# First token group of an mLSTM and SwiGLU kernel: its own results in two halves of 64 tokens, and a new order ahead of the feed-forward part

## The chip, the cores and the metric

The kernel runs on one core of a Trainium2 chip. A core has five engines that run side by side, each with its own queue of instructions: TensorE (PE: matmuls and transposes, results into PSUM), VectorE (DVE), ScalarE (ACT), GpSimd (POOL) and SyncE (SP, which here only issues DMAs). They wait for one another by semaphores. The metric is the device time of one execution in microseconds (us); all times are in us where nothing else is said.

## What is computed

Two blocks in sequence, all in float32. The first is an mLSTM cell over 4 batches, 8 heads, 768 tokens and head dimension 40; the second is a SwiGLU feed-forward over the 3072 tokens with 320 features.

```python
for t in range(S):                                   # S = 768, for all batches and heads
    m_new = np.maximum(f_gate[:, :, t] + m, i_gate[:, :, t])
    f_stab = np.exp(f_gate[:, :, t] + m - m_new)
    i_stab = np.exp(i_gate[:, :, t] - m_new)
    m = m_new
    C = f_stab[..., None, None] * C + i_stab[..., None, None] * np.einsum('bhd,bhe->bhde', vt, kt)
    n = f_stab[..., None] * n + i_stab[..., None] * kt
    h_tilde = np.einsum('bhde,bhe->bhd', C, qt)
    denom = np.maximum(np.abs(np.einsum('bhd,bhd->bh', n, qt)[:, :, None]), 1.0)
    y[:, :, t] = sigmoid(o_gate[:, :, t]) * h_tilde / denom
x = y.transpose(0, 2, 1, 3).reshape(B * S, H * D)    # 3072 x 320
g = x @ w_gate                                       # 320 x 1536
out = (g * sigmoid(g) * (x @ w_val)) @ w_out         # 1536 x 320
```

The weights of the feed-forward arrive as 64-bit floats and are turned into 32-bit floats on the chip.

## The kernel before

**Groups and stages.** The 768 tokens are cut into 6 groups of 128 tokens, and the recurrence becomes matrix products: a group's result is the part that its own tokens give each other (a masked 128 x 128 matrix of weights for every batch and head) and a part from the state C that earlier groups left. Group 0 has no earlier state, so it needs its own part alone. A group's results, transposed (`xT`), feed `hidden` (L646), which makes twelve slices of 128 of the 1536 hidden features, and `project` or `project_all`, which multiply by w_out. From the first `hidden` on, TensorE works on the feed-forward of one group, and the cell of the next group is put between its slices. What lies ahead of the first `hidden` is the cell of group 0 and the conversion of the first pieces of the weights. The change is almost wholly there, in L567 to L614.

**Pairs.** The 32 combinations of batch and head (`BH`) are worked on in two halves P = 0 and 1, each of two batches u = 2P and 2P + 1 with 8 heads.

**Group 0, in the order of its functions:**
- `first_mask`, `first_inputs`, `first_maxima` (L478 to L490) sum the logarithms of the decay weights in eight PSUM banks; `first_exp` takes exp of them into `W0[s, t]` (128 source tokens s on the partitions, 128 result tokens t). For s > t the weight is 0. `W0` lies in the buffer `h_sb`, which the hidden features use later, and which takes weight pieces in between.
- `first_turn` (L504) transposes k or q of one half, 128 tokens at a time: eight transposes of 128 x 128 in two banks, and a copy from each bank to SBUF, on the engines given. `turn_one` (L291), which later groups use, does the same 64 tokens at a time, with 64-row transposes, and copies each half of the tokens.
- `first_values` (GpSimd) weights v by the last column of `W0` for the state that group 0 leaves. It must come ahead of `first_scores` of the same half.
- `first_scores` multiplies q and k in 64 matmul records over both halves, and VectorE multiplies them into `W0` (L523).
- `first_own(u)` multiplies `W0` by v for the 8 heads of a batch, over all 128 source tokens, into the bank `first_y` (L530). Column 41 of v is 1 and gives the denominator.
- `first_x(u)` on VectorE divides, `sig(P)` on ScalarE takes the sigmoid of the output gate, `first_gate(P)` multiplies by it and copies 64 columns behind the row.
- `first_seam(P)` transposes the two batches' results (five blocks each, three banks) and copies them into `xT(0)`.
- `first_state(P)` multiplies k and the weighted v (L552), and `first_kept` copies the product to the state buffer.

**Weights.** `piece_load(p)` issues the DMAs of piece p of the weights, the w_gate half on SP's queue and the w_val half on ScalarE's for the first five pieces. Pieces 0 and 1 go to buffers of their own; piece 2 goes to part of `h_sb` and so waits until `first_own(2)` has read `W0` there. `convert(j)` is `scale(j)` (two ops on ScalarE, the upper and the lower word), `join(j)` (two on VectorE) and `rounded(j)` (one, on VectorE or GpSimd).

**`late_sums`** (L273) sums the forget gates of the later groups (a scan on VectorE, and a memset and a subtraction on GpSimd); `late_maxima`, after the first slice of `hidden`, uses it. **`burn(n)`** issues n matmuls of constants, whose results nobody reads.

**What sets the order.** The order of the calls is the order in each engine's queue; nothing is rescheduled. PSUM has eight banks under two names, "cell" and "gen", four each, given out in turn: a new tile waits until the readers of the fourth last one of its name are done. `hidden` takes its banks from "gen".

## Time and profile before

| | us |
|---|---|
| median of 3 runs (552.24 to 552.7) | 552.34 |
| the profiled execution | 551.99 |
| its span, first to last instruction | 550.0 |
| first matmul of `hidden` starts | 32.04 |
| `first_own` of batch 0, 1, 2, 3 starts | 14.49, 18.63, 23.09, 25.23 |
| scores of the first and the second half start | 12.44, 20.44 |
| first and second seam start on TensorE | 26.93, 29.45 |
| o_gate issues of both halves (SP) | 14.44 to 19.38 |
| w_gate and w_val halves of piece 0 issued | 19.43, 18.40 |
| piece 2 issued, on both queues | 25.04 |

The page of a profile gives busy time by engine, then the span in 40 slices, the DMA queues, the chain of work that ended last, and groups of instructions (line, engine, operation, what it writes and reads, shape, count, busy time and mean duration, idle time before it and what ended it). "PEld" is the loading of weights into TensorE's array, which overlaps its matmuls. A matmul in float32 leaves two records, a transpose one. Matmuls are pipelined, so that the ends in the records are modelled: the starts say how fast they follow each other. The timeline merges consecutive records of one line; its columns are start, length, engine and line, operation and operands, shape and count.

Slices of the page's second part, the first tenth of the span in the first four digits:

```profile
PE   8999999999999999999999999999999999999997
PEld 4964556774555575545575545576455567444475
DVE  5778668961346232455421545531436621111100
ACT  4376755352110133011024101115110100111100
POOL 2304265673011060011133011124001100000000
```

## The change

- `first_own` makes each head's product in two parts: result tokens 64 to 127 from all 128 source tokens, and result tokens 0 to 63 from source tokens 0 to 63 (the rest of their weights is 0). There are 16 matmuls for a batch instead of 8.
- The second half's k and q are turned by `turn_one`, k into banks of the name "gen".
- `first_own(1)` stands between these two turns, `first_x(0)` behind both.
- `piece_load(1)` follows `piece_load(0)`, ahead of `sig(0)`.
- `first_state(0)` moves from behind the second seam to ahead of the first, into a "gen" bank.
- The first half's gate goes to GpSimd; `sig(1)` and the second half's gate stand behind the first bank of the first seam.
- `late_sums` moves behind `convert(1)`; `rounded(0)` moves ahead of the second seam; both state copies are on ScalarE.
- The burns are 3, 2, 2, 2 and 5 instead of 3, 2 and 1.
- `scale` is written as two functions that are called one after the other, as before.

```diff
-    def turn_one(P, src, dst, engs):
-        tp = [bank("tp_kq").rearrange("p (a t) -> p a t", t=SUB) for _ in range(2)]
+    def turn_one(P, src, dst, engs, tag="cell"):
+        tp = [bank("tp_kq", tag).rearrange("p (a t) -> p a t", t=SUB) for _ in range(2)]
...
         for h in range(H):
-            nc.tensor.matmul(first_y[u][:, h, :], lhsT=W0[:, u * H + h, :], rhs=v_sb[:, u * H + h, :], start=True, stop=True)
+            n = u * H + h
+            nc.tensor.matmul(first_y[u][half(1), h, :], lhsT=W0[:, n, half(1)], rhs=v_sb[:, n, :], start=True, stop=True)
+            nc.tensor.matmul(first_y[u][half(0), h, :], lhsT=W0[half(0), n, half(0)], rhs=v_sb[half(0), n, :], start=True,
+                             stop=True)
...
-    def first_gate(P):
+    def first_gate(P, eng):
         for u in (2 * P, 2 * P + 1):
             x = x_sb[:, u, 0:DM].rearrange("p (h d) -> p h d", d=D)
-            nc.vector.tensor_tensor(x, x, o_sb[:, u * H:(u + 1) * H], op=ALU.mult)
+            eng.tensor_tensor(x, x, o_sb[:, u * H:(u + 1) * H], op=ALU.mult)
...
-    def first_seam(P, engs):
+    def first_seam(P, engs, between={}):
...
             copy(eng, xT(0)[:, c:c + len(cs), 2 * P * L:(2 * P + 2) * L].rearrange("p c (u s) -> p c u s", u=2), tp)
+            for f in between.get(c, ()):
+                f()
...
     first_own(0)
-    late_sums()
-    first_turn(1, k_sb, kT, (A, A))
+    turn_one(1, k_sb, kT, (A, A), "gen")
+    first_own(1)
+    turn_one(1, q_sb, qT, (A, V))
     first_x(0)
-    first_turn(1, q_sb, qT, (A, V))
     load(o_sb, o_gate, 0, 1)
     piece_load(0)
-    first_own(1)
+    piece_load(1)
     first_values(1)
+    burn(3)
     first_scores(1)
     first_x(1)
     sig(0)
-    piece_load(1)
-    burn(3)
+    burn(2)
     first_own(2)
     piece_load(2, h_sb[:, 1:1 + NKC])
-    sig(1)
     burn(2)
     first_own(3)
-    first_gate(0)
+    ps0 = first_state(0, "gen")
+    burn(2)
+    first_gate(0, G)
     first_x(2)
     first_x(3)
-    first_gate(1)
-    first_seam(0, (A, A, V))
+    first_seam(0, (A, A, V), {0: [run(sig, 1), run(first_gate, 1, V)]})
     scale(0)
     ps1 = first_state(1, "gen")
-    burn(1, "gen")
+    burn(5)
     piece_load(3, h_sb[:, NH - NKC:])
     join(0)
+    rounded(0, V)
     first_seam(1, (A, A, V))
-    rounded(0, V)
-    first_kept(0, first_state(0), A)
-    first_kept(1, ps1, V)
+    first_kept(0, ps0, A)
+    first_kept(1, ps1, A)
     convert(1, V)
+    late_sums()
```

## What was predicted, before the changed kernel had run

> **What bounds the kernel now.** I read the page's engine shares and its chain first, then the chain in order of time up to the first feed-forward matmul, then the TensorE timeline where its matmuls change shape, then the groups by form, last the landings.

> ```profile
> PE 544.9 (99%) x4989; PEld 311.4 (57%) x4989; DVE 236.1 (43%) x397; ACT 136.1 (25%) x203; POOL 103.0 (19%) x95
> PE 98%; DVE 1%; ACT 0%; issue 0%; ACTq 0%; DVEq 0%
> ...
> 18.79 1.71 PE first_y L530 x16
> 20.51 1.99 PE sp L519 x32
> 22.49 0.76 PE burn L469 x3
> 23.25 1.71 PE first_y L530 x16
> 24.96 0.43 PE burn L469 x2
> 25.39 1.73 PE first_y L530 x16
> ...
> 32.04 0.66 PE gv_ps L651
> ```

> TensorE is the bound. From 32.04, where the first matmul of `hidden` (L651) starts, it has next to no gaps, and the change touches almost nothing after that. So the question is only when L651 starts. Before it TensorE is the chain until 27.12, with each `first_own` at 1.7; then VectorE's division, gate and weight join lead to 32.04.

> Now the shape of the matmuls: "128*64" is rows*columns of the array that one of them uses.

> ```profile
> 27.62 0.60 PE L564 MATMUL tp_x<-ident,x_sb 128*128 128x128 f32 x4
> 28.15 0.32 PE L552 MATMUL add<-vw_sb,k_sb 128*64 128x41 f32 x4
> ...
> 28.82 0.47 PE L552 MATMUL add<-vw_sb,k_sb 128*64 128x41 f32 x10
> 29.22 0.39 PE L469 MATMUL burn<-junk 128*128 128x512 bf16 x1
> ...
> 48.53 1.03 PE L651 MATMUL gv_ps<-xT,wgv_sb 64*128 64x512 f32 x4
> 49.48 0.49 PE L625 MATMUL tp_g<-ident,i_sb 32*128 32x32 f32 x5
> 49.82 0.47 PE L625 MATMUL tp_g<-ident,keep 32*128 32x32 f32 x5
> 50.22 0.70 PE L651 MATMUL gv_ps<-xT,wgv_sb 64*128 64x512 f32 x2
> ```

> Within one shape matmuls overlap: four of 273 ns end in 0.60, so one starts every 0.11. Where the shape changes, the next starts only 0.07 before the last one's modelled end: 28.22 to 28.15, 29.29 to 29.22, 49.56 to 49.48, 50.29 to 50.22. The last two change the rows alone and pay it too.

> ```profile
> L530 PE MATMUL first_y<-v_sb,h_sb 128*128 128x41 f32 x64 | 7.8, 279 | 0.2 <-DVE h_sb L523 0.2
> L552 PE MATMUL add<-vw_sb,k_sb 128*64 128x41 f32 x64 | 2.3, 231 | 0.0
> DMA to landing us min/median/max: 4.7/6.8/8.8
> ```

> An f32 matmul leaves two records (64 for 32 heads). The last line is of the first weight piece (issues from 18.4 and 19.43): its w_gate half lands 8.8 after 19.43, at 28.27.

> [...]

> **The change part by part.**

> *`first_own` in two parts.* Each head had one 128*128 matmul (two records, 0.112 apart, so 1.79 an own). Now it has one of 128*64 and one of 64*64, alternating, so the shape changes twice a head. The trace doesn't show this alternation. From below: if changing costs nothing, it is 32 short records like `add`, 0.95. From above, by the rule just read: second record 0.08 after the first (four `add` records in 0.32, each 0.23), next shape 0.23 - 0.07 = 0.16 later. A head is 2 x (0.08 + 0.16) = 0.48, an own 3.84. I take 3.84, because every change of shape in the trace pays, whichever side of it changes; rows alone change 128 to 64 here, but columns move as well. A softer bound is 2.4, if only one of the two changes drains.

> *Turns of the second pair on 64 rows.* `turn_one` runs later in both kernels: 16 records in 0.50 (59.57 to 60.06) against 1.09 for 8 of 128 rows. It saves 0.6 a turn, but both halves of the tokens must be copied before any score, where the old form needed its first copy alone.

> *Order and waits*, on the profile's clock:
> - own(0): its second head starts at 15.04 as before (it waits for VectorE's weighted scores). 15.04 + 7 x 0.48 = 18.40.
> - k turn 0.50 and a change 0.09: 18.99. own(1): 22.83. The transposed k was copied by ScalarE long before.
> - q turn: 0.66 to its modelled end, 23.49. ScalarE copies 0.59, VectorE 0.69: 24.21. burn(3), 0.65, lies in this wait. Scores start 24.25 (20.44 before).
> - Scores 2.01 (20.437 to the burn at 22.45): 26.26. VectorE's weighting starts 1.26 after the scores' start (20.44 to 21.70), and its second op ends at 26.8.
> - burn(2) 0.43 and a change 0.11: 26.80. own(2): 30.64. burn(2): 31.18. own(3): 35.02.
> - first_state(0), moved here: 0.90 for its 32 records plus a change, 1.07: 36.09. burn(2): 36.52.
> - First seam: its first copy is ready 0.67 after the start (26.93 to 27.61): 37.19. ScalarE copies (the next starts 0.48 later), then sig(1) of 0.74, now placed behind it: 38.41. VectorE's gate of the second pair waits for that, 0.88: 39.32. Copy of the seam's last part, 0.42: 39.66.
> - Join and rounding: 0.49 + 0.83 + 0.83 with 0.03 and 0.14 between: 42.02. L651 follows 0.14 later: 42.16.

> ScalarE's scale of that piece starts at 38.8 by its queue and ends before VectorE asks at 39.7. The second seam follows burn(5) at about 39.9, and ScalarE has copied it by 41.7, so neither is last.

> Sum: 42.16 - 32.04 = +10.12. By parts: four owns +8.2, eight more burns +1.7, turns -1.2, the rest is the waits for copies and for sig(1).

> *Edits at nothing.* The first gate on GpSimd: two ops of 0.74 (L362, 128x328) and the 0.29 copy, done by about 31 beside own(3); on the path only if the owns were short. `late_sums` behind the second convert: VectorE's 1.47 fits the 1.96 that it idles before L657; GpSimd's 0.62 and 1.53 lie in its 13.9 idle to 43.4. Uncovered, it would cost up to 1.5. Both `first_kept` on ScalarE: 0.43 more, before the second scale, 2 ahead of need; if that goes, 0.4.

> *DMA queues.* ScalarE's two w_val issues (0.68, 0.61) now stand together ahead of sig(0), but behind a q copy that is 5 later; landing takes about 5, so 29 against a need at 38.8. Piece 2 waits for own(2), to 30.8 instead of 25.0. Behind it on SP's queue stand pieces 3 to 5 and the next k, M_dram and q loads: they move by 6 while their users move by 10. They cost nothing, and if they did, it would be the 2 to 3 that the DMA engines, full at 30, may be late.

> **Rivals.**
> 1. *The change of shape is cheap* (an own is 0.95). [...] Against: every change read above. Then the q turn waits for its data at 17.7, scores start at 19.2, the owns end at 24.0, and VectorE and ScalarE are ready at 28; the landing at 28.27 decides. From it 0.03 + 0.83 + 0.03 + 0.49 + 0.03 + 0.83 + 0.14 + 0.83 + 0.14 = 3.35: L651 at 31.6, -0.4. This is the other side: no slower, about 551.9, and it decides if a head takes under 0.15 (31 heads on the path: 42.16 - 31 x 0.33 = 31.9).
> 2. *The same, with the landing worse.* The second w_val half is issued right after the first and piece 2 at 23, so both can be ahead of the w_gate half. Its 640 KB at the 200 GB/s moved then is 3.2: +2.8, 555.2. Against: SP issues that half first.
> 3. *One change of the two drains*: an own of 2.4, -5.8 against the forecast, 556.7.
> 4. *The clock falls.* [...] At half clock a head's 0.23 of loads and passes doubles: 8 x 0.23 = 1.9 an own; for two owns +3.7, 566.2. Against: the array isn't idle, and burns stand between.

> **How the numbers follow.** The profiled execution took 551.99, 550.0 of it span; the median of the runs is 552.34, 0.35 more. 551.99 + 10.12 = 562.1; on the median 562.5. Its own range is 560.0 to 563.5: if the change takes 0.13 instead of 0.16 (a 40-column `add` is 0.196 long, and L651 follows it at 154.26, again 0.07 before its end), a head is 0.41 and the sum falls by 2.2; the upper end is a wait of 1 that I missed.

> Chances: forecast 0.66, rival 1 0.09, rival 2 0.05, rival 3 0.12, rival 4 0.08. The range 556.5 to 565.0 takes in rival 3 and leaves out 1, 2 and 4. Faster or slower counts from 0.2%, 1.1 us, about what a measurement can tell. Rival 1 is mostly within it: faster 0.01, same 0.08, slower 0.91.

> **What would show it.** In the new profile the two lines of `first_own` should have matmuls without idle time, an own of 3.8, and each record's start 0.16 after one of the other shape. Scores of the second pair near 24.3, the first L651 near 42.2, the span from there to the end unchanged at 518. The forecast is wrong if an own takes 1 us: then L651 stands at 31 to 32 and its wait ends with the weight join after a DMA landing. If the granted clock is below full after 5 us, rival 4 is at work.

## The result, and the profile after

The changed kernel takes 573.38 us (median of four runs, 572.18 to 574.48) against 552.52 for the kernel before in the same session: a ratio of 1.0377, 95% interval 1.035 to 1.0405, or +20.9. The forecast was slower, by 10.1, with a range up to 565.0. The direction is right, the size is about half of what came.

The row of the page with the granted clock of TensorE over the span, in 40 slices of 14.3 us, shows that something new happened. The first row is of the kernel before, with a 9 in every slice; in the second, of the changed kernel, the second to fourth slice (14 to 57) have 6, 6 and 8:

```profile
PEclk9999999999999999999999999999999999999999
```

```profile
PEclk9668999999999999999999999999999999999999
```

The table by stretches of the changed kernel says where. The columns are the stretch in us, then busy time and instructions of TensorE, its weight loads, VectorE, ScalarE and GpSimd, then the granted clock, the DMA share and GB/s:

```profile
15.00:17.00 2.00, 2.00 (x19) 1.57 (x18) 0.98 (x2) 0.00 (x0) 0.00 (x0) 1.00 1.46 150
17.00:18.00 1.00, 1.00 (x9) 0.84 (x8) 0.00 (x0) 0.00 (x0) 0.00 (x0) 0.81 0.67 88
20.00:25.00 5.00, 5.00 (x29) 3.90 (x30) 0.00 (x0) 0.66 (x2) 0.71 (x1) 0.50 1.06 180
...
31.00:32.00 1.00, 1.00 (x9) 0.41 (x8) 0.64 (x2) 0.00 (x0) 0.00 (x0) 0.86 0.13 20
...
34.00:35.00 1.00, 1.00 (x10) 0.78 (x9) 0.00 (x0) 0.00 (x0) 0.94 (x2) 0.85 0.00 0
38.00:43.00 5.00, 5.00 (x29) 3.96 (x28) 0.00 (x0) 0.00 (x0) 0.00 (x0) 0.50 1.00 216
...
48.00:49.00 1.00, 1.00 (x31) 0.98 (x30) 0.90 (x3) 1.00 (x3) 0.00 (x0) 0.83 1.04 197
```

The clock is 1.00 in all but the end of `first_own(0)`, falls to 0.50 between 17 and 18, comes back between 31 and 32, falls again between 34 and 35 and comes back between 48 and 49. The mixed stretches give the moments: 0.81 is 0.38 us at half clock, so it fell at 17.62; 0.86 puts the return at 31.28, 0.85 the second fall at 34.70, 0.83 the second return at 48.34. The distances are 13.66, 3.42 and 13.64: 4, 1 and 4 times 3.41. TensorE is marked busy almost all through (5.00 of 5.00 from 20 to 25, 3.78 of 4.00 from 44 to 48). That is the point for a reader of such pages: "busy 9" and "clock 0.50" stand beside each other.

The timeline of TensorE in the changed kernel, with one head of `first_own` at full clock, the start of the last head of batch 0, one head at half clock, and the larger steps behind it:

```profile
15.32 0.31 PE L542 MATMUL first_y<-v_sb,h_sb 128*64 128x41 f32 x2
15.56 0.31 PE L543 MATMUL first_y<-v_sb,h_sb 64*64 64x41 f32 x2
15.79 0.31 PE L542 MATMUL first_y<-v_sb,h_sb 128*64 128x41 f32 x2
...
17.70 0.43 PE L542 MATMUL first_y<-v_sb,h_sb 128*64 128x41 f32 x2
...
20.21 0.43 PE L542 MATMUL first_y<-v_sb,h_sb 128*64 128x41 f32 x2
20.57 0.43 PE L543 MATMUL first_y<-v_sb,h_sb 64*64 64x41 f32 x2
20.93 0.43 PE L542 MATMUL first_y<-v_sb,h_sb 128*64 128x41 f32 x2
...
27.73 3.73 PE L530 MATMUL sp<-qT,kT 64*128 64x128 f32 x32
...
43.06 1.93 PE L566 MATMUL add<-vw_sb,k_sb 128*64 128x41 f32 x32
...
51.76 8.85 PE L668 MATMUL gv_ps<-xT,wgv_sb 64*128 64x512 f32 x40 [0.19 <-DVE wgv_sb L217]
```

At full clock a head takes 0.47 (15.32 to 15.79) where the forecast had 0.48. At half clock it takes 0.72, the scores take 3.7 instead of 2.0, the state sums 1.9 instead of 1.1. The first matmul of `hidden` (L668, L651 before) starts at 51.76: 19.72 later than before, where 10.12 was forecast.

Against the forecast's own timetable, us from the span's start:

| Step | Forecast | Measured | Longer by |
|---|---|---|---|
| own(0) ends | 18.40 | 18.43 | 0.03 |
| k turned, own(1) starts | 18.99 | 19.48 | 0.46 |
| own(1) ends | 22.83 | 25.29 | 1.97 |
| q turned and copied, scores start | 24.25 | 27.73 | 1.02 |
| own(2) starts | 26.80 | 31.93 | 1.65 |
| own(2) ends | 30.64 | 36.27 | 0.50 |
| own(3) starts | 31.18 | 37.24 | 0.43 |
| own(3) ends | 35.02 | 43.06 | 1.98 |
| state sums and burns, seam starts | 36.52 | 45.75 | 1.19 |
| hidden starts | 42.16 | 51.76 | 0.37 |

The sum of the last column is 9.60, and nearly all of it is in steps that ran at half clock. That the first step agrees to 0.03 is luck in part: its second head starts 0.20 earlier than forecast (14.84, not 15.04), and its last head, from 17.70, is already at half clock and takes 0.73. What supports the forecast's own is the head of 0.47 at full clock. After L668 the span is another 2.4 longer than before (22.1 in all): 1.22 up to the fifth step of `hidden` and 1.16 spread over the first group's projection and the second group.

## The experiments

The question was what the loss is made of: the changes of tile shape, the clock, or the new order with its waits and loads. Times are medians, ratios against the kernel before in the same session (552.3 to 552.8), with the 95% interval.

**e1, the own whole again.** The changed kernel, with:

```diff
-            nc.tensor.matmul(first_y[u][half(1), h, :], lhsT=W0[:, n, half(1)], rhs=v_sb[:, n, :], start=True, stop=True)
-            nc.tensor.matmul(first_y[u][half(0), h, :], lhsT=W0[half(0), n, half(0)], rhs=v_sb[half(0), n, :], start=True,
-                             stop=True)
+            nc.tensor.matmul(first_y[u][:, h, :], lhsT=W0[:, u * H + h, :], rhs=v_sb[:, u * H + h, :], start=True, stop=True)
```

> The changed kernel with first_own whole again (one 128*128 matmul a head); order, turns, waits and burns as changed. Theory A (the split own is the loss: its changes of shape cost 0.16 each and its emptiness halves the granted clock, and what follows runs at half clock): an own is 1.79, the granted clock stays at 1.00 after 5 us, scores of the second pair take 2.0, the first L668 stands near 34 and the time is 554 to 556 (2 at L668 for the eight more burns and the wait for sig, 1.2 for the late conversions at m=2 and m=3). Theory B (the new order, its waits and its DMA issues are the larger part): L668 stays above 43 and the time above 565.

Measured: 558.01, ratio 1.0098 (1.0078 to 1.0118). Of the 20.9, 15.4 go with the split, so theory B falls; but L665 (the first matmul of `hidden`) stands at 36.96 and not at 34, and the time lies in neither theory's range. From the timeline, then the table by stretches, of e1:

```profile
17.09 3.29 PE L541 MATMUL first_y<-v_sb,h_sb 128*128 128x41 f32 x16
```

```profile
17.00:18.00 1.00, 1.00 (x12) 0.93 (x9) 0.00 (x0) 0.81 (x2) 0.00 (x0) 0.75 0.71 96
18.00:20.00 2.00, 2.00 (x12) 2.00 (x11) 0.00 (x0) 0.27 (x1) 0.72 (x1) 0.50 1.21 200
...
24.00:25.00 1.00, 1.00 (x18) 1.00 (x18) 0.25 (x1) 0.86 (x2) 0.05 (x1) 0.84 1.16 192
```

The clock fell here too, from 17.5 to 24.3, with owns of the old form. So the new order alone is enough to lose the clock, and theory A was right about the split and incomplete about the clock.

**e2, the split alone.** The kernel before, with the split in place of its one line, and nothing else:

```diff
-            nc.tensor.matmul(first_y[u][:, h, :], lhsT=W0[:, u * H + h, :], rhs=v_sb[:, u * H + h, :], start=True, stop=True)
+            nc.tensor.matmul(first_y[u][half(1), h, :], lhsT=W0[:, n, half(1)], rhs=v_sb[:, n, :], start=True, stop=True)
+            nc.tensor.matmul(first_y[u][half(0), h, :], lhsT=W0[half(0), n, half(0)], rhs=v_sb[half(0), n, :], start=True,
+                             stop=True)
```

> The kernel before with nothing but first_own split into 128*64 and 64*64 matmuls, alternating. Theory A: owns of 3.84 at full clock and 5.8 at half, the clock at 0.5 in several stretches between 17 and 45; the first matmul of hidden, 32.04 before, stands at 44 to 50 and the time is 565 to 571. Theory C (the clock falls only because the new order leaves TensorE waiting): clock 1.00, four owns of 3.84, so 552.5 + 8.2 = 560 to 561. Theory B: below 556.

Measured: 567.05, ratio 1.0256 (1.0224 to 1.0288), first matmul of `hidden` at 47.69. The table by stretches of e2:

```profile
16.00:18.00 2.00, 2.00 (x19) 1.61 (x18) 2.00 (x3) 0.00 (x0) 0.00 (x0) 1.00 1.33 152
...
35.00:43.00 8.00, 8.00 (x42) 6.42 (x42) 2.21 (x8) 1.12 (x2) 0.00 (x0) 0.50 0.98 189
```

As theory A said: the clock falls in the old order too, and the split alone costs 14.5. Theory C (only the new order starves TensorE) falls.

**e3 and e4, the split without its changes of shape.** Both are the changed kernel with another `first_own`. e3 runs the eight matmuls of 128\*64 and then the eight of 64\*64; e4 gives both halves 128 rows (the lower 64 rows of the first half's weights are zeros, so this only adds work). First e3's edit, then e4's:

```diff
             nc.tensor.matmul(first_y[u][half(1), h, :], lhsT=W0[:, n, half(1)], rhs=v_sb[:, n, :], start=True, stop=True)
+        for h in range(H):
+            n = u * H + h
             nc.tensor.matmul(first_y[u][half(0), h, :], lhsT=W0[half(0), n, half(0)], rhs=v_sb[half(0), n, :], start=True,
                              stop=True)
```

```diff
-            nc.tensor.matmul(first_y[u][half(1), h, :], lhsT=W0[:, n, half(1)], rhs=v_sb[:, n, :], start=True, stop=True)
-            nc.tensor.matmul(first_y[u][half(0), h, :], lhsT=W0[half(0), n, half(0)], rhs=v_sb[half(0), n, :], start=True,
-                             stop=True)
+            for i in (1, 0):
+                nc.tensor.matmul(first_y[u][half(i), h, :], lhsT=W0[:, n, half(i)], rhs=v_sb[:, n, :], start=True, stop=True)
```

> The changed kernel with the same matmuls in first_own, ordered otherwise: first the eight of 128*64, then the eight of 64*64, so one change of shape inside an own instead of fifteen. Theory A: an own is 0.95 plus one or two changes, 1.1 to 1.4, the clock stays 1.00, L668 stands at 31.5 to 34, the time is 552 to 555. Theory D (small tiles as such keep TensorE too empty, whatever their order): the clock still falls to 0.5 in the owns, an own is near 2 and the time is 558 or more.

> The changed kernel with both halves of first_own as 128*64 matmuls (the first half's lower 64 rows hold zeros from the mask, so the same sums come out): no change of shape inside an own, and a little more work than e3_grouped. Theory A: an own is 0.95 to 1.0, clock 1.00, L668 at 31.5 to 34, time 552 to 555, equal to e3_grouped within 0.6. Theory D: the clock falls and the time is 558 or more. If it is the change of rows alone that costs, this one is as fast as e3_grouped or faster; if it is the change of column half, an own stays at 3.8.

Measured: e3 558.88, ratio 1.0114 (1.0093 to 1.0134); e4 554.95, ratio 1.0048 (1.0031 to 1.0064); the clock is 1.00 in both. Here are own(1) of e3 and own(1) of e4 with its first matmul of `hidden`, from their timelines:

```profile
18.34 1.13 PE L542 MATMUL first_y<-v_sb,h_sb 128*64 128x41 f32 x16
19.39 1.12 PE L545 MATMUL first_y<-v_sb,h_sb 64*64 64x41 f32 x16
```

```profile
16.39 1.13 PE L543 MATMUL first_y<-v_sb,h_sb 128*64 128x41 f32 x32
...
32.48 17.92 PE L667 MATMUL gv_ps<-xT,wgv_sb 64*128 64x512 f32 x80 [1.91 <-DVE wgv_sb L217]
```

e4's 32 records end in 1.13, so an own is 1.07 long instead of 1.79 for the whole one. That is close to the forecast's lower bound (0.95), and with it 18.4 of the 20.9 are gone. In e4 the column half changes with every matmul and the rows don't, and an own is short; so what costs here is the change of rows between 128 and 64 from one matmul to the next. My size for e3 was wrong: its own is 2.1, not 1.1 to 1.4, and e4 is 3.9 faster than e3 and not equal to it. That e3's own and time (near 2, 558 or more) are those of theory D is a coincidence, since D has them from a fallen clock and e3's is 1.00. Sixteen records on one half of the columns take 1.05, as long as 32 whose matmuls alternate between the halves: on alternate halves they follow each other twice as fast.

In e4 the forecast's first rival can be read as well, although its premise was false for the kernel as changed. The w_gate half landed at 29.16 (its reader waits for it, timeline of e4):

```profile
29.18 0.80 ACT L190 ACTIVATE top<-raw 128x640 f32<-128x640 f32 x1 [0.34 <-DMA raw<-in_moe_w_gate_dram]
```

L667 follows 3.3 later; the rival's sum from the landing was 3.35.

**f1, work added inside the owns.** The changed kernel, with the split as it is and 24 matmuls more on the path:

```diff
                              stop=True)
+            if h in (2, 5):
+                burn(3)
```

Measured: four runs of 569.62, 571.42, 575.69 and 575.98, with mean granted clocks of 1.000, 0.997, 0.985 and 0.985. The profiled one is the first, the fastest of the four. Its table by stretches and its timeline:

```profile
24.00:34.00 10.00, 9.70 (x95) 6.64 (x97) 5.04 (x13) 2.61 (x3) 2.01 (x3) 1.00 0.46 91
34.00:48.00 14.00, 13.27 (x140) 9.28 (x140) 5.10 (x14) 4.22 (x8) 0.30 (x1) 1.00 0.83 160
```

```profile
48.42 8.00 PE L670 MATMUL gv_ps<-xT,wgv_sb 64*128 64x512 f32 x36 [0.93 <-DVE wgv_sb L217]
```

With the clock kept, L670 stands at 48.42 (48.5 expected), 3.3 earlier than the changed kernel with its less work. An own here is 5.32 (20.77 to 26.09), and 16 steps of 0.238 are 3.81, so the burns are 1.51 an own; 48.42 less four of these is 42.4, against the forecast's 42.16 for full clock. Theory E falls for this run; e1 speaks against it too, where the clock fell with whole owns. The median, 573.56, doesn't show it and lies outside the expected 569 to 572: two of the four runs lost the clock for long all the same and took 6 more, and a third lost a little of it and took 1.8 more. The burns were cut too fine; the runs with the lower clock are the longer ones.

**f2, one edit that keeps e1's clock.** e1 with two burns more:

```diff
     first_own(0)
+    burn(2)
     turn_one(1, k_sb, kT, (A, A), "gen")
```

> e1_own_whole with burn(2) behind first_own(0). There the window from 14.1 to 17.5 streamed 0.23 by the same reckoning and the clock fell until 24.3. Theory A: two burns lift it by 0.12 to 0.35, the clock stays at 1.00, own(1) takes 1.8 instead of 3.3, the scores 2.0 instead of 2.7, L665 stands at 34 to 35 instead of 36.96, the time is 555 to 556.3. Theory F (e1's fall has another reason, such as the wait before its second head): clock as in e1, 558 to 559.

Measured: 556.1, ratio 1.0066 (1.0051 to 1.008). The timeline of f2:

```profile
17.76 1.98 PE L541 MATMUL first_y<-v_sb,h_sb 128*128 128x41 f32 x16
...
34.73 8.85 PE L666 MATMUL gv_ps<-xT,wgv_sb 64*128 64x512 f32 x40 [0.94 <-DVE wgv_sb L217]
```

The clock is 1.00 and the numbers of theory A are met, the own(1) to 0.1 (17.76 to 19.67): two matmuls of some 0.2 each, with nothing to compute, bring 1.9. This is what the new order, with these two burns, costs without any loss of clock: L666 at 34.73, 2.7 later than before.

**h1, late_sums at its old place.** The forecast had counted this edit at nothing. On f2:

```diff
     first_own(0)
+    late_sums()
     burn(2)
...
     convert(1, V)
-    late_sums()
```

> f2_whole_and_burn with late_sums behind first_own(0) again, as in the kernel before. Theory L (late_sums was not free: in f2 VectorE's L209 of the third piece took 1.28 instead of 0.50 while GpSimd ran L286 beside it, and the first hidden stage's steps to m=2 and m=3 were 4.67 and 4.70 instead of 4.29 each): both steps are 4.29 again, L209 takes 0.5, and the time falls by 0.8 to 555.0 to 555.6. Theory M (the pieces arrive later and that is the wait): the steps stay at 4.6 to 4.7 and the time at 556.

Measured: 555.19, ratio 1.0059 (1.0043 to 1.0076). VectorE and GpSimd in the timeline of f2, then VectorE in that of h1:

```profile
39.99 1.54 POOL L286 TENSOR_TENSOR i_sb<-i_sb,f_sb 32x640 f32<-32x640 f32 x1
...
40.61 1.28 DVE L209 TENSOR_SCALAR wgv_sb<-top 128x640 uint32<-128x640 uint32 x1
```

```profile
40.47 0.49 DVE L209 TENSOR_SCALAR wgv_sb<-top 128x640 uint32<-128x640 uint32 x1
```

While GpSimd subtracts, VectorE's shift takes 1.28 instead of 0.49. The third and fourth step of `hidden` then wait for their weights: between the starts of its steps stand 4.36, 4.67 and 4.70 in f2, and 4.37, 4.29 and 4.29 in h1, as in the kernel before (4.37, 4.29, 4.29). Theory L holds by the trace: the two steps are 0.79 shorter together, and that is the price. The times alone wouldn't show it, since the two ratios (1.0066 and 1.0059) have intervals that overlap. The shift ends at 41.89, 0.36 after GpSimd's subtraction (41.53). By what means the one slows the other isn't shown here.

The kernel before showed the same already, in its timeline, where the shift takes 1.14 beside another operation of GpSimd and 0.46 to 0.50 elsewhere:

```profile
57.77 1.55 POOL L207 TENSOR_TENSOR wgv_sb<-wgv_sb,low 128x640 int32<-128x640 int32 x1 [2.55 <-DVE wgv_sb L200]
...
58.53 1.14 DVE L199 TENSOR_SCALAR wgv_sb<-top 128x640 uint32<-128x640 uint32 x1 [0.91 <-ACT top L190]
```

**f3, the good form of the split in the kernel before.** The kernel before with e4's `first_own`, no more:

```diff
-            nc.tensor.matmul(first_y[u][:, h, :], lhsT=W0[:, u * H + h, :], rhs=v_sb[:, u * H + h, :], start=True, stop=True)
+            for i in (1, 0):
+                nc.tensor.matmul(first_y[u][half(i), h, :], lhsT=W0[:, n, half(i)], rhs=v_sb[:, n, :], start=True, stop=True)
```

> The kernel before with nothing but first_own as two 128*64 matmuls a head, both over all 128 rows (same sums). An own falls from 1.79 to about 1.07, four of them by 2.9. Theory G (the landing of the first weight piece's w_gate half at 28.27 and the 3.3 of VectorE and ScalarE behind it are the next limit): the first L654 stands at 31.5 to 31.8 and the time is 0.1 to 0.6 less than before. Theory H (TensorE's owns are the limit in the first 28 us): L654 near 29.5 and the time 549.5 to 550.5.

Measured: 554.73, ratio 1.0038 (1.0024 to 1.0051). The owns are 1.07, and the kernel is slower for it. From the table by stretches of f3:

```profile
30.00:33.00 3.00, 0.60 (x8) 0.37 (x6) 2.97 (x6) 3.00 (x6) 0.00 (x0) 1.00 1.06 279
...
34.00:36.00 2.00, 2.00 (x6) 0.81 (x4) 0.90 (x2) 0.79 (x2) 0.00 (x0) 0.50 1.03 339
```

and from its timeline:

```profile
32.55 12.70 PE L653 MATMUL gv_ps<-xT,wgv_sb 64*128 64x512 f32 x50 [2.40 <-DVE wgv_sb L207]
```

Theory G was right that the landing decides: TensorE is done early and waits 2.40 for the weight join. It was wrong in its sizes: the landing itself came at 29.13 instead of 28.27, so that `hidden` starts later than before, and the time rose by 2.2 instead of falling. And the wait has a second price that no theory named: after it the clock is 0.50 for 3.4 us, and the first step of `hidden` takes 6.07 instead of 4.37. What moved the landing by 0.86 was not tested; piece 2's load, which waits for own(2), is issued 1.7 earlier here (23.30 instead of 25.04).

**g1, the same with the wait filled.** On f3:

```diff
     rounded(0, V)
+    burn(7)
     first_kept(0, first_state(0), A)
```

> f3_before_one_shape with burn(7) ahead of first_state(0). In f3 the shorter owns left TensorE without work for 2.4 before the first hidden matmul (32.55), and the clock was 0.5 from 33.49 to 36.9, so that m=0 took 6.07 instead of 4.36. Theory A: seven burns (1.5 of streaming in the window of 3.41 that ends near 33.5) keep the clock at 1.00, m=0 takes 4.36 again, the first hidden matmul stays at 32.5 to 32.7 (its wait for the weight join is what holds it) and the time falls by 1.7 to 552.8 to 553.3. Theory J (the clock fell there for another reason, such as the start of the long matmuls): m=0 at 6 again, 554.5 to 555.

Measured: 553.11, ratio 1.0006 (0.9997 to 1.0015), the clock 1.00, `hidden` from 32.70, its first step 4.39. The same stretch as above, in g1:

```profile
34.00:36.00 2.00, 2.00 (x12) 0.97 (x10) 1.83 (x3) 1.97 (x3) 0.00 (x0) 1.00 1.06 199
```

Seven matmuls on junk data bring 1.6. With the wait filled the clock stays, so its loss in f3 came from the wait, and theory J falls.

**f4 and g2, the best of both.** f4 is e4 with two edits to the order undone; g2 adds `burn(4)` behind the second seam, between the two `first_kept`. The edit of f4:

```diff
     first_own(0)
+    late_sums()
...
     piece_load(0)
-    piece_load(1)
...
     sig(0)
+    piece_load(1)
...
     convert(1, V)
-    late_sums()
```

> e4_one_shape with two of the edits to the order undone: piece_load(1) stands behind sig(0) again, so that its second w_val half is not issued ahead of the first piece's w_gate half, and late_sums stands behind first_own(0) again. Theory G: the w_gate half lands near 28.3 instead of 29.16, the first hidden matmul stands at 31.6 instead of 32.48, the wait at m=3 (0.4) is gone, and the time is 552.2 to 553.3. Theory I (the rest of e4's 2.3 lies in other edits, such as the gate on GpSimd or sig(1) behind the seam): 554 or more.

> f4_one_shape_loads_back with burn(4) behind the second seam, in the 0.94 that TensorE waits there for the weight join. Two of 22 runs of f4 had a clock of 0.997 and took 556.6. Theory A: these no longer occur, the first hidden matmul stays within 0.3 of 31.82, the median is 553 to 553.8, no better than the kernel before: what is left above it lies in waits after the first group's hidden stage. Theory K (the prologue can still give): 552 or less.

Measured: f4 553.79, ratio 1.0028 (1.0018 to 1.0038), first matmul of `hidden` at 31.82 (32.48 in e4) and its steps at 4.29 again; g2 553.5, ratio 1.0016 (1.0004 to 1.0027), 31.99. f4's time lies between the two theories' ranges. It enters the hidden stage 0.2 ahead of the kernel before and is 1.2 behind at the end of the span, lost in short stops of the projection and of the second group that differ from profile to profile. What causes these was not settled. One of g2's 14 runs still had a clock of 0.997 and took 556.2, so that part of its expectation failed.

No version here beats the kernel before. In f3 and e4 it is the first weights' landing that holds `hidden`. In f4 it isn't: the w_gate half lands at 27.24, earlier than expected, and what leads to `hidden` in f4's chain are the five burns, the second seam, its copy and the last part of the weight join, from the critical view of f4:

```profile
28.61 1.19 PE burn L479 x5
29.79 0.45 PE tp_x L577 x4
...
30.27 0.59 ACT xT L121
30.86 0.82 DVE wgv_sb L217
...
31.82 13.58 PE gv_ps L667 x61
```

Whether fewer burns at this place would let `hidden` start earlier, and keep the clock, was not tried.

## Why the prediction was right and where it failed

- *The bound, and that only the start of `hidden` matters*: right for 19.72 of the 22.1 of span. The forecast's "unchanged at 518" after it was 2.4 short. Of that, 1.22 is VectorE held up beside the moved `late_sums`, in the third and fourth step of `hidden`: the waits of f2 and h1 (0.8), and 0.4 more because here VectorE's L210 took 2.05 instead of 0.83 beside GpSimd's L286. The rest is stops that weren't traced to a cause.
- *The change of shape costs 0.16, an own 3.84*: right. A head took 0.47 at full clock, and f1's path at full clock comes to 42.4 where the forecast had 42.16. e4 shows the other side: with the rows kept, an own is 1.07. The working had read changes of shape from four places, two with columns alone changing and two with rows alone; in the split it is the rows.
- *Rivals 1 to 3* (change of shape cheap, or only one of two): fell with the first head.
- *The step that failed is the full clock.* The forecast's sum runs the whole path at full clock and puts the loss of it at nothing, as rival 4, with a chance of 0.08. The runs showed 8 windows of 3.41 at half clock in the profiled execution, in two stretches of four, and 9.60 on the path to `hidden`. Rival 4's own figure was short as well: its doubling of an own was right in size (1.9 expected, 1.97 and 1.98 measured), but it counted two owns and nothing else, 3.7. Once lowered, the clock stayed low and whatever ran then paid: the turns (0.46 for k), the scores (1.65), the state sums and seam (1.19).
- *The reason against rival 4*, "the array isn't idle, and burns stand between", is what was wrong in kind: the clock fell with TensorE marked busy (2.00 of 2.00 from 15 to 17 and 1.00 of 1.00 from 17 to 18, the fall at 17.62). What fits the runs is how much of a window of 3.41, the length from the distances above, data streams through the array. This is an estimate: a step of 20 records of 512 columns takes 4.29, so a column is 0.42 ns and 41 columns are 0.017; a split own streams 32 of these, 0.55 in 3.84, or 14%. A whole own streams 16 in 1.79, about the same share. In the kernel before that did no harm; it is half as long, and its neighbours are denser (the window from 15.24 to 18.65 comes to 32% by the same estimate).
- *late_sums, "costs nothing"* failed: the time slots were free, as the forecast said, but VectorE's work took longer beside GpSimd's, 0.8 in f2, as it did at 58.53 in the kernel before.
- *The sum for the order* (burns +1.7, turns -1.2, waits) is about right: f2, with whole owns and the clock at 1.00, is 2.7 later at `hidden`, where the forecast less its owns' 8.2 says 1.9; f2's two burns more are 0.4 of the difference.

How much of the 20.9 is whose, roughly: an own at full clock is 3.81 in f1's clean run and in e2 (eight heads of 0.476) and was 1.79, so the slower owns are some 8; the table's 9.6 in the profiled run is the clock; the rest, some 3, is the order and late_sums, which f2 alone puts at 3.6 with its two burns more.

## What to carry to other kernels

Before splitting a matmul into smaller tiles, ask two things of the trace: do rows stay the same from one matmul to the next (an own took 1.07 with the rows kept and 3.81 with the rows changing, both at full clock), and how much of any 3.4 us does the array really stream. If the second falls toward a quarter (the estimate from these runs, see below), price what follows at half clock too, and not the thin stretch alone: here it stayed low for one to four windows of 3.41 (one in f3, two in e1, four in the changed kernel). A stage made faster can get there by waiting, as in f3 (a wait of 2.40, then 3.4 at a clock of 0.50). Read the granted clock beside the busy time from the start.

## What the runs showed of the hardware that was not expected

- The lowered clock comes in whole windows. Twice the lost share of clock times the span is the time at half clock: the changed kernel's four runs had mean clocks of 0.976, 0.979, 0.982 and 0.985, so 27.5, 24.0, 20.5 and 17.1, or 8, 7, 6 and 5 windows of 3.41; they took 574.48, 574.32, 572.44 and 572.18, so a window has no fixed price. Why the same program falls into a different number of them was not tested. The place of the windows against the program may be a reason, since it differs between two executions: the trace's record of the full clock begins 5.00 after the start of the span in the kernel before and 3.97 in the changed kernel, where every later change lies a whole number of windows of 3.41 behind it (17.63, 31.28, 34.69 and 48.35 are 4, 8, 9 and 13).
- With the windows placed by that record, the reckoning above (columns of all records that start, an estimate) sorts them. The six at whose end the clock fell (two of the changed kernel, two of e2, one of e1 and one of f3) streamed 14 to 25%, e1's from 14.08 to 17.49 among them with 23%. Those of the kernel before, all at full clock, streamed 32% or more from 10 us to the last 10 us; the leanest is the one from 15.24 to 18.65. The edge isn't settled by this: a window from 14.28 in the kernel before would stream 21%, and none of its 69 runs with a clock on record has a mean under 0.999, where one window at half clock would make it 0.997. What brings the clock back isn't sorted by the same reckoning.
- Matmuls of 128\*64 on alternate column halves start every 0.033; on the same half every 0.066; with rows changing between 128 and 64, two records every 0.24. (e4, e3 and the changed kernel.)
